# Loading x in pieces of 118 partitions, a scratch array with four rows side by side, and routing lists that stand earlier in the order

## The chip, the cores and the metric

The kernel runs on one core of one Trainium2 chip. The metric is the device time of one execution in microseconds (us). Five engines work side by side, each through its own instructions in order: TensorE (PE, with PEld for its weight loads), VectorE (DVE), ScalarE (ACT), GpSimd (POOL) and SyncE (SP). SP and ACT issue plain DMAs, POOL issues the indexed ones (gather and scatter by row number). All of them are carried out by the core's 16 DMA engines.

## The reference

The reference smooths each sequence with a causal filter and then routes every token to one of eight experts.

```python
# x: (8, 3584, 192) f32, 8 heads of 24 channels, 7 taps per head
w = softmax(weight, axis=-1)
attn[b, s] = sum over k of w[head, k] * x[b, s - 6 + k]        # zeros before s = 0

# 28672 tokens of 192, 8 experts with room for 3584 tokens each
logits = attn @ w_gate                                          # 28672 x 8
# greedy: all (token, expert) pairs by falling logit; a pair is taken
# if the token has no expert yet and the expert still has room
out[token] = relu(attn[token] @ w1[e]) @ w2[e]                  # 192 -> 1024 -> 192
```

Everything is float32. The kernel computes the matrix products of the experts in split halves (a high and a low part of each operand), which is why one product shows as several matmuls.

## The kernel before

**Convolution.** The 28672 tokens are handled in 16 half batches of 1792. A half batch lies in SBUF as a tile `X` of 118 partitions x 16 columns x 192: column w holds the 112 tokens of run w on partitions 6 to 117, and on partitions 0 to 5 the six tokens ahead of them (the halo). `load` (L182 to L192) fills it with two DMAs on SP's queue, one for the six halo partitions and one for the other 112. Each run that such a DMA moves is one token row of 768 bytes. `conv` (L194 to L203) makes one matmul `cv<-X,TH` for each of the 8 heads (TH holds the filter as a band matrix), ACT copies each result to the tile `a`, and a DMA on ACT's queue writes `a` to the scratch array `attn` in DRAM, token by token. There are three buffers for `X` and two for `a`: a load waits for the matmuls that used its buffer, and the copies of half batch i wait until the write of half batch i - 2 has landed.

**Logits.** DVE transposes `a` (`transp`), 48 small matmuls `pl` make the logits, ACT copies them (`L`), PE turns them (`pt`) and DVE writes them to `LT`, with a correction `pm` for columns that hold no token. `end` does the turn and the running maximum (`top`). In the loop the transposes of half batch i - 1 and the logits of i - 2 stand between the matmuls of half batch i.

**Routing in the background.** `Route` makes the lists of token numbers by expert. Its steps are generators, run one after the other by `Steps`, which is asked at many places of the loops (`hook`) whether the next step's input should be there. This is judged by `Pace`, a small clock that adds estimated times of the instructions written so far. The first list (`half(0)`: a threshold, then places, slots, a sort with the one-hot tiles `oa`, a gather by matmul and the numbers `ia0`) covers the first 128 of 256 columns, that is the first eight half batches. `tail` and `tail2` then compute the logits of half batches 14 and 15, and `half(1)`, `rest` and `last` make the other lists during the experts' work.

**Experts.** `FFN` works through 56 tiles of 512 tokens. For each, POOL gathers four times 128 rows of `attn` by the list (L1175), PE transposes them (`px`), `l1` makes eight blocks `ph`, and `l2` sums them to `y`, whose rows POOL scatters to the output (L1243). Weights come through four buffers `raw` (`wload`, SP's queue) and are split by `wsplit` into a high part (ACT) and a low part (POOL or DVE). The first tile's gather stands behind the whole convolution and waits for `ia0`.

The order of each engine is the order in which this program writes its instructions; there is no later scheduler.

Of the kernel before, what the change touches and what calls it, by code (L numbers as in the profile page):

```python
# [16 lines left out]
G = 256  # L17
# [95 lines left out]
def build(ctx, tc, nc, x, weight, wg, attn, LT, wk):  # L113
# [48 lines left out]
    pm = wk.tile([128, 16], F32, name="pm")  # L162

    def gate_ops():
        for pb in range(4):
            nc.sync.dma_start(wgr[32 * pb:32 * pb + 32], wg.rearrange("(c f) e -> f c e", f=32))
        P.memset(GF, 0.0)
        for pb in range(4):
            q = slice(32 * pb, 32 * pb + 32)
            P.tensor_copy(GF[q, :, 8 * pb:8 * pb + 8], wgr[q])  # L170

        pi = cst.tile([128, 1], I32, name="pi")
        P.iota(pi, pattern=[[0, 1]], base=0, channel_multiplier=1)
        V.tensor_scalar(pi, pi, 16, None, op0=OP.bitwise_and)
        V.memset(pm, 0.0)
        for b in range(4):
            V.tensor_scalar(pm[:, 4 * b + 3:4 * b + 4], pi, -1.0 / 16, None, op0=OP.mult)
# [16 lines left out]
    def conv(i, mid):  # L194
# [8 lines left out]
        A.dma_start(attn[i * 1792:(i + 1) * 1792].rearrange("(w p) d -> p w d", p=W), a[0:W])  # L203
# [10 lines left out]
    def transp_last(u):  # L214

        i = NHB - 1
        a = wk.tile([128, 16, 64], F32, name="X%d" % u)
        for q in range(2):
            V.transpose(a[:, 8 * q:8 * q + 8], AA[i][:, 8 * q:8 * q + 8, 64 * u:64 * u + 64])
        AT[i] = AT[i] + [a] if u else [a]  # L220

    def logits(i, u):
# [4 lines left out]
        for c in range(4):  # L227
            w = slice(4 * c, 4 * c + 4)
            t = AT[i][u // 2].rearrange("p w (c t) -> p w c t", t=32)[:, w, u % 2] if i == NHB - 1 else AT[i][0][:, w, u]
            PE.matmul(pl[32 * c:32 * c + 32, 0:128], GF[:, u], t, start=(u == 0), stop=(u == 5))  # L230
# [13 lines left out]
    k.toeplitz, k.gate_ops, k.transp_last = toeplitz, gate_ops, transp_last  # L244
# [4 lines left out]
TA = 12  # L249
# [13 lines left out]
class Route:  # L263

# [268 lines left out]
    def tokens(self, nt, idx, e1=8, t1=None):  # L533
# [10 lines left out]
        i = v(wk.tile([128, 128], I32, name="m_j"))  # L544
        off = wk.tile([128, 1], F32, name="off")
# [16 lines left out]
    def lists(self, F, nt, h, base, idx, *part):  # L562
# [6 lines left out]
        yield from self.tokens(nt, idx, *part)  # L569
# [240 lines left out]
class General:  # L810


    def __init__(self, ctx, tc, ltab, attn, w1, w2, out, ident, drm):
# [4 lines left out]
        self.list = drm.tile([NTOK, 1], I32, name="glist")  # L818

    def consts(self):  # L820
# [20 lines left out]
        self.idi = p.tile([128, G], I32, name="g_idi")  # L841
        V.tensor_copy(self.idi, self.id)
# [131 lines left out]
    def lists(self):  # L974
# [25 lines left out]
        i1 = p.tile([128, 1], I32, name="g_i1")  # L1000
        with tc.For_i(0, G, 1) as g:
            V.tensor_copy(s1, si[:, bass.ds(g, 1)])
            V.tensor_copy(i1, self.idi[:, bass.ds(g, 1)])
# [4 lines left out]
    def ffn(self):  # L1008
# [5 lines left out]
        ix = p.tile([128, 1], I32, name="g_ix")  # L1014
# [7 lines left out]
        with tc.For_i(0, NE, 1) as e:  # L1022
# [3 lines left out]
            with tc.For_i(0, CAP // 128, 1) as t:  # L1026
                nc.sync.dma_start(ix, self.list[bass.ds(e * CAP + t * 128, 128)])
                P.indirect_dma_start(out=x, out_offset=None, in_=self.attn,
                                     in_offset=bass.IndirectOffsetOnAxis(ap=ix, axis=0),
# [15 lines left out]
                P.indirect_dma_start(out=self.out, out_offset=bass.IndirectOffsetOnAxis(ap=ix, axis=0),  # L1045
# [8 lines left out]
class FFN:  # L1054
# [235 lines left out]
    def run(self, idx_of, at, eng, free):  # L1290
# [4 lines left out]
        for i in range(n + 1):  # L1295
            at(i)
            if i + 2 < n:
                self.gather(i + 2, idx_of(tiles[i + 2]))
# [18 lines left out]

NL = 3


def moe_kernel(ctx, tc, x, weight, wg, w1, w2, out):
# [6 lines left out]
    with ExitStack() as cw:  # L1328
# [16 lines left out]

        order = [(e, (0,)) for e in range(NE)]
# [10 lines left out]
        def half(h):  # L1357
# [6 lines left out]
            yield from r.lists(r.F, TA, h, 0 if h else None, *((ia,) if h else (ia0, 8, 4)))  # L1364

        def rest():
# [3 lines left out]
            yield from r.lists(r.F, TB, 1, None, ib0, NL, 4)  # L1370

        def last():
            yield from r.lists(r.F, TB, 0, 1, ib)

        def tail():

            for u in range(6):
                k.logits(14, u)
                if u % 2:
                    yield PEA if u == 5 else None  # L1380
            end(14)
            cs.close()
            ff.wpool2(cw, 1)
            ff.hp[1] = pool(cw, "fh1", 1, **late)
            yield

        def tail2():
# [5 lines left out]
            nc.sync.dma_start(r.ltab, LT)  # L1393
            yield
# [4 lines left out]
        cx = [ExitStack() for _ in range(3)]  # L1399
        k = build(cs, tc, nc, x, weight, wg, attn, LT, wk)  # L1400
# [3 lines left out]
        k.ap = pool(ca, "ap", 2, **right)  # L1404
# [13 lines left out]
        def first(e):  # L1418
# [136 lines left out]
```

## Time and profile before

| | us |
|---|---|
| median of three runs (1328.0 to 1332.42) | 1328.93 |
| the profiled execution, its own time | 1324.88 |
| span of that profile | 1323.1 |
| last write of `attn` issued | 170.06 |
| first matmul of the first expert tile (`ph<-xa,w`) | 181.96 |
| PE busy in the span | 1251.3 |

PE is busy for 95% of the span. Two stages differ: up to about 170 us the convolution runs while 23 MB of x are read and 22 MB of scratch are written, and the DMA engines are nearly always busy; from 182 us on, the experts' matmuls fill PE, and DMA is busy for a quarter to a half of the time. In the page's second part a digit is the busy share of a slice in tenths; a DMA share above 1 in a row of a window means that recorded packets overlap. Packets are counted over all 16 DMA engines of the core.

### The profile page before, as it was taken

What the parts mean: (1) busy time and instruction counts of PE and PEld (TensorE: products, weight loads), DVE (VectorE), ACT (ScalarE), POOL (GpSimd) and SP (SyncE); (2) the same over time, 40 slices, a digit from 0 to 9 for tenths busy, and PEclk for the clock granted to TensorE, in tenths of its full rate; (3) what the DMA queues carried; (4) which work ended last, traced back from release to release, by engine and by line L of the source; (5) the groups of instructions that cost most, each with busy time, mean ns of one, the idle gap of its engine ahead of it and who ended that gap; (6) DMA issues with size and microseconds to landing.
All of it is one profiled execution on the core that took longest, in us unless ns stands there. A gap on an engine that the chain in (4) does not pass through costs nothing.

```text
span 1323.1 us, 21760 instructions
## 1 busy us (share of the span) xinstructions
PE 1251.3 (95%) x7879; PEld 1077.4 (81%) x7879; DVE 1005.2 (76%) x2223; ACT 543.2 (41%) x1182; POOL 540.1 (41%) x547
## 2 busy tenths in 40 slices
PE   5888959999799999999999999999999999999997
PEld 2444637887789888888899999999999999999996
DVE  7369648779999988899757777777777777777772
ACT  4434434475444434443333333333333333333332
POOL 3000065586644434435224434444444444444422
PEclk9889989899899999999899999999999999999999
DMA  9999879488753433424222341432323222141100
GB/s 239 285 294 297 231 211 324 154 275 270 241 186 101 143 99 134 145 91 143 76 83 89 130 160 45 149 101 87 104 87 104 93 93 90 48 148 46 41 29 27
DMA packets 114434, 188.29 MB, mean 142 GB/s; under 512 B 12352, under 2 KB 86544, under 8 KB 110096
## 3 DMA queue, kind: packets, MB, share of 16 engines
q1 hardware_dynamic: 63888, 120.75, 28.4%
q0 software_dynamic: 21504, 44.07, 10.9%
q10 hardware_dynamic: 28928, 22.02, 5.2%
q8 instruction: 63, 1.03, 0.3%
q14 instruction: 51, 0.42, 0.1%
HBM read 114.44 MB, written 72.35 MB: 141 GB/s over the span
## 4 chain that ended last, share of the span: by engine, by line
PE 77%; DVE 9%; DMA 8%; issue 2%; POOL 2%; ACT 2%; SPq 1%; POOLq 0%; ACTq 0%; DVEq 0%
PE ph L54 34%; PE y L54 33%; DMA attn<-a 5%; PE cv L54 4%; PE bg L54 3%; DMA raw<-in_moe_w_dram 3%; DVE X L54 2%; DVE hl L54 2%; PE px L54 1%; PE pl L54 1%; DVE TH L54 1%; DVE oa L54 1%; POOL xg L1175 1%; POOL w L1156 1%; DVE r_w L54 0%
## 5 line engine op out<-in xcount | busy, mean ns | idle before, releaser
L54 PE MATMUL y<-w,hh 128*128 128x384 f32 x1792 | 543.6, 359 | 0.0
L54 ACT ACTIVATE hh<-ph 128x512 fp32r<-128x512 f32 x448 | 267.0, 596 | 492.3 <-PE ph L54 491.9
L54 PE MATMUL y<-w,hl 128*128 128x192 f32 x1792 | 451.3, 252 | 0.0
L54 DVE SCALAR_TENSOR_TENSOR hl<-ph,hh 128x512 fp32r<-128x512 f32 x448 | 308.2, 689 | 174.6 <-ACT hh L54 170.9
L54 PE MATMUL ph<-xa,w 128*128 128x512 f32 x1344 | 399.7, 406 | 2.3 <-DVE hl L54 2.3
L54 PEld LDWEIGHTS y<-w,hh 128*128 128x128 f32 x1792 | 339.4, 189 | 25.2 <-issue 7.5
L54 PEld LDWEIGHTS y<-w,hl 128*128 128x128 f32 x1792 | 344.0, 192 | 15.2
L1243 POOL DMA_INDIRECT out_dram<-yo,ib x128 | 128.0, 1000 | 294.2 <-DVE yo L54 279.4
L54 PEld LDWEIGHTS ph<-xa,w 128*128 128x128 f32 x1344 | 221.5, 191 | 22.7 <-DVE hl L54 2.9
L1243 POOL DMA_INDIRECT out_dram<-yo,ia x96 | 106.3, 1108 | 241.0 <-DVE yo L54 210.3
L54 DVE STREAM_TRANSPOSE xs<-xg 32x256 f32<-32x256 f32 (+1 forms) x512 | 188.8, 369 | 8.8
L54 PE MATMUL ph<-xd,w 128*128 128x512 f32 x448 | 179.7, 401 | 0.0
L54 PE MATMUL ph<-xd,dl 128*128 128x512 f32 x448 | 175.8, 392 | 1.2 <-DVE dl L54 1.2
L1175 POOL DMA_INDIRECT xg<-attn,ib x128 | 129.7, 1013 | 40.1 <-issue 39.8
L54 PE MATMUL cv<-X,TH 118*128 118x384 f32 x256 | 103.8, 539 | 31.1 <-ACT a L54 18.4
L1175 POOL DMA_INDIRECT xg<-attn,ia x96 | 106.8, 1112 | 28.9 <-issue 23.2
L54 ACT ACTIVATE yt<-y 128x192 f32<-128x192 f32 x224 | 73.3, 327 | 108.2 <-PE y L54 105.2
L54 DVE TENSOR_TENSOR yo<-y,yt 128x192 f32<-128x192 f32 x224 | 79.7, 356 | 42.1 <-ACT yt L54 39.3
L54 PEld LDWEIGHTS ph<-xd,dl 128*128 128x128 f32 x448 | 85.1, 190 | 21.6 <-DVE dl L54 2.6
L54 PEld LDWEIGHTS cv<-X,TH 118*128 118x128 f32 x256 | 48.0, 206 | 66.0 <-ACT a L54 26.7
L54 PEld LDWEIGHTS ph<-xd,w 128*128 128x128 f32 x448 | 85.2, 190 | 20.1 <-DVE xd L54 0.7
L54 ACT ACTIVATE a<-cv 128x384 f32<-128x384 f32 x128 | 59.2, 491 | 66.2 <-DMA attn<-a 36.8
(230 smaller groups left out, 966.6 us busy)
## 6 DMA issues: line engine op xcount, KB each, us to landing
w<-kw SPq DMA_DIRECT2D x16, 1536.0 KB
w<-kv SPq DMA_DIRECT2D x16, 1536.0 KB
X<-in_x_dram SPq DMA_DIRECT2D x16, 1344.0 KB
attn<-a ACTq DMA_DIRECT2D x16, 1344.0 KB
kw<-w SPq DMA_DIRECT2D x48, 256.0 KB
kv<-w SPq DMA_DIRECT2D x32, 384.0 KB
raw<-in_moe_w_dram SPq DMA_DIRECT2D x32, 192.0 KB
raw<-in_moe_w_dram SPq DMA_DIRECT2D x16, 256.0 KB
```

The source lines that it names most:

```text
L54: return f(*a, **k)
L1156: eng.tensor_tensor(lo, r[0:n], hi[0:n].bitcast(F32), op=OP.subtract)
L1175: self.nc.gpsimd.indirect_dma_start(out=t[:, b], out_offset=None, in_=self.attn[0:rows], in_offset=bass.IndirectOffsetOnAxis(ap=idx[b], ax ...
L1243: st = nc.gpsimd.indirect_dma_start(out=self.out, out_offset=bass.IndirectOffsetOnAxis(ap=idx, axis=0), in_=o, in_offset=None, bounds_chec ...
```

## The change

**Loads of x.** `load` now moves all 118 partitions at once, in four DMAs of four columns each. In an even half batch, whose first column has no halo in DRAM, that column goes by itself over 112 partitions and the next DMA takes three columns. The same rows as before are moved, 768 bytes each.

**Scratch.** The row order of `attn` becomes: half batch, group of four runs, token within a run, run within the group. So the four columns of a group lie side by side and one run of the write is 3072 bytes. A gather needs the scratch row and the scatter the token number, so `tokens` computes both (`ja`, `ia`), and the slow general path keeps pairs. `a` has three buffers.

**Order.** Transposes and logits of half batch i - 1 stand within half batch i. From half batch 13 on they are held back until the first list is done; `hook` tells `Pace` a time (8.6 per half batch, 11.0 at the start). The first two tiles' gathers are issued as soon as `ia0` and `ja0` are there, and the first tile's transposes stand inside half batch 15. The pools for them are opened at the start. `tail` (half batch 14) is gone from the background, since its logits belong to the loop now; half batch 15 keeps a tail. The first tile's buffer is cleared by POOL, not DVE.

**Small moves.** The correction `pm` is added by ACT when it copies the logits (two copies in place of one), and ACT instead of DVE writes `LT`.

SP's order at the start of the program: `wb` are the filter taps, `X` the half batches, `wgr` the gate weights. Before:

```order
L123 DMA wb<-in_weight_dram 128x56
L188 DMA X<-in_x_dram 6x15x192
L192 DMA X<-in_x_dram 112x16x192
L191 DMA X<-in_x_dram 6x16x192
L192 DMA X<-in_x_dram 112x16x192
L166 DMA wgr<-in_moe_w_gate_dram 32x6x8 x4
```

Now:

```order
L124 DMA wb<-in_weight_dram 128x56
L190 DMA X<-in_x_dram 112x192
L193 DMA X<-in_x_dram 118x3x192
L193 DMA X<-in_x_dram 118x4x192 x7
L167 DMA wgr<-in_moe_w_gate_dram 32x6x8 x4
```

Two half batches take nine DMAs in place of four, and eight of the nine have 118 partitions as their outer count.

POOL's order from its last clearing of `X` to the second tile's weights (`w`, `dl` are low parts of split weights, `xg` the gathered tokens). Before:

```order
L187 MEMSET X 6x192 x4
L1078 MEMSET dl 64x1024
L1156 TENSOR_TENSOR w_1629<-raw,w_1629 128x512
L1156 TENSOR_TENSOR dl<-raw,w_1629 64x512
L1175 DMA xg<-attn,ia_105 128x192 x8
L1156 TENSOR_TENSOR w_1629<-raw,w_1629 128x512
L1156 TENSOR_TENSOR dl<-raw,w_1629 64x512
L1078 MEMSET dl 64x1024
```

Now:

```order
L189 MEMSET X 6x192 x4
L1179 MEMSET xg 128x768
L1181 DMA xg<-attn,ja_109 128x192 x4
L1179 MEMSET xg 128x768
L1181 DMA xg<-attn,ja_109 128x192 x4
L1162 TENSOR_TENSOR w_1622<-raw,w_1622 128x512
L1162 TENSOR_TENSOR dl<-raw,w_1622 64x512
L1162 TENSOR_TENSOR w_1622<-raw,w_1622 128x512
L1162 TENSOR_TENSOR dl<-raw,w_1622 64x512
L1084 MEMSET dl 64x1024
```

The eight gathers of the first two tiles moved ahead of all weight work on POOL.

ACT's order over the last two half batches (`asm` belongs to the first list, `w<-raw` are weights of the first expert). Before:

```order
L54 ACTIVATE asm<-bg 128x192
L54 ACTIVATE a<-cv 128x16x24 x2
L54 ACTIVATE w_1629<-raw 128x512
L54 ACTIVATE a<-cv 128x16x24
L54 ACTIVATE L<-pl 128x128
L54 ACTIVATE w_1629<-raw 128x512
L54 ACTIVATE a<-cv 128x16x24 x3
L203 DMA attn<-a 112x16x192
```

Now, from `asm` to the middle of half batch 14:

```order
L55 ACTIVATE asm<-bg 128x192
L55 ACTIVATE a<-cv 128x16x24 x3
L204 DMA attn<-a 112x4x768
L55 ACTIVATE a<-cv 128x16x24
L55 ACTIVATE w_1622<-raw 128x512
L55 ACTIVATE a<-cv 128x16x24 x2
L55 ACTIVATE w_1622<-raw 128x512
L55 ACTIVATE a<-cv 128x16x24 x2
L55 ACTIVATE L<-pl 128x4x16
L55 ACTIVATE L<-pl,pm 128x4x16
L55 ACTIVATE w_1622<-raw 128x512
```

The last matmul of the first list moved from half batch 15 to half batch 13, and the copies of half batch 14 now stand behind weights that come through `raw`.

The core of the diff:

```diff
@@ load
+        x_ = lambda w, n, p: bass.AP(tensor=x.tensor, offset=o + (w * W + p - 6) * D, ap=[[D, 118 - p], [W * D, n], [1, D]])
+
+        parts = [(4 * c, 4) for c in range(4)]
         if hf == 0:
             P.memset(t[0:6, 0], 0.0)
-            nc.sync.dma_start(t[0:6, 1:16], bass.AP(tensor=x.tensor, offset=o + (W - 6) * D,
-                                                    ap=[[D, 6], [W * D, 15], [1, D]]))
-        else:
-            nc.sync.dma_start(t[0:6], bass.AP(tensor=x.tensor, offset=o - 6 * D, ap=[[D, 6], [W * D, 16], [1, D]]))
-        nc.sync.dma_start(t[6:118], bass.AP(tensor=x.tensor, offset=o, ap=[[D, W], [W * D, 16], [1, D]]))
+            nc.sync.dma_start(t[6:118, 0:1], x_(0, 1, 6))
+            parts[0] = (1, 3)
+        for w, n in parts:
+            nc.sync.dma_start(t[:, w:w + n], x_(w, n, 0))
@@ conv
-        A.dma_start(attn[i * 1792:(i + 1) * 1792].rearrange("(w p) d -> p w d", p=W), a[0:W])
+        A.dma_start(attn[i * 1792:(i + 1) * 1792].rearrange("(g p b) d -> p g (b d)", g=4, b=4),
+                    a[0:W].rearrange("p (g b) d -> p g (b d)", b=4))
@@ logits, logits_t
-            A.activation(L, pl[:, 0:128], AF.Copy)
+            l, m = (t.rearrange("p (w t) -> p w t", t=32) for t in (L, pl[:, 0:128]))
+            A.activation(l[:, :, 0:16], m[:, :, 0:16], AF.Copy)
+            A.activation(l[:, :, 16:32], m[:, :, 16:32], AF.Identity, bias=pm)
...
-        V.tensor_tensor(o, v, pm.rearrange("p (b q) -> p b q", q=4)[:, None].to_broadcast([128, 8, 4, 4]), op=OP.add)
+        A.activation(o, v, AF.Copy)
@@ tokens
+        V.scalar_tensor_tensor(y, i, -127.0 / 4, x, op0=OP.mult, op1=OP.add)
...
+        V.scalar_tensor_tensor(y, gi, 28.0, y, op0=OP.mult, op1=OP.add)
...
+        V.scalar_tensor_tensor(y, i, 4.0, y, op0=OP.mult, op1=OP.add)
+        V.tensor_scalar(row, y, 4.0, None, op0=OP.mult)
@@ moe_kernel
+PERIOD, START = 8.6, 11.0
+LAG = 13
...
-        bg = Steps(nc, r, (half(0), tail(), tail2(), half(1), rest(), last()))
-        bg.keep = 5
+        bg = Steps(nc, r, (half(0), tail(), half(1), rest(), last()))
+        bg.keep = 4
...
-        k.ap = pool(ca, "ap", 2, **right)
+        k.ap = pool(ca, "ap", 3, **right)
...
+        def steps(i):
+
+            def gate(u):
+                if u == 3:
+                    return end(i)
+                for f in range(2 * u, 2 * u + 2):
+                    k.logits(i, f)
+
+            return [partial(k.transp, i, u) for u in range(4)] + [partial(gate, u) for u in range(4)]
+
+        def hook(at):
+            nc.pe = max(nc.pe, PERIOD * at / 8 + START)
             bg.hook(1.5)
-            if len(bg.gens) == 5:
-                gather()
+            if not got and len(bg.gens) == 4:
+                first()
+                got.append(at)
+            elif got and at >= got[0] + 10 and at % 8 in (2, 5) and todo:
+                for _ in range(2):
+                    todo.pop(0)()
...
             def mid(h):
-                if i and h < 4:
-                    k.transp(i - 1, h)
-                if 2 <= i and h in (2, 5):
-                    for u in range(3):
-                        k.logits(i - 2, h // 4 * 3 + u)
-                if i == 15 and h in (4, 5):
+
+                if i and h == 0:
+                    left.extend(steps(i - 1))
+                for _ in range(2 if got else 1):
+                    if left and (i < LAG or got):
+                        left.pop(0)()
+                    if not left or left[0].func != k.transp:
+                        break
+                if i >= 14 and h % 2:
                     ff.wsplit(-1, P)
...
```

More of the change, by code (lines that the diff above doesn't have):

```diff
@@ L568, in lists @@
         yield from self.gather(nt, base is None)
-        yield from self.tokens(nt, idx, *part)
+        yield from self.tokens(nt, idx, row, *part)
     def counts(self, n0):
@@ L1369, in rest @@
             yield from r.final(NL)
-            yield from r.lists(r.F, TB, 1, None, ib0, NL, 4)
+            yield from r.lists(r.F, TB, 1, None, ib0, jb0, NL, 4)
         def last():
-            yield from r.lists(r.F, TB, 0, 1, ib)
+            yield from r.lists(r.F, TB, 0, 1, ib, jb)
         def tail():
[L1377 to L1387, printed above, removed]
             for u in range(6):
@@ L1490, in moe_kernel, with idx_of @@
         ff.op = pool(cw, "fo", 3, **late)
+        ff.xp = pool(cw, "fp", 1, **late)
         ff.hp = [pool(cw, "fh0", 1, **late), None]
         ff.wpool(cw, 1)
-        def idx_of(tile_):
+        def idx_of(tile_, rows=False):
             e, t = tile_[1]
             if t == 0:
-                return [ia0[:, e, b:b + 1] for b in range(4)]
+                return [(ja0 if rows else ia0)[:, e, b:b + 1] for b in range(4)]
             if t < 3:
@@ L1500, in idx_of @@
                     bg.drain(2)
-                return [ia[:, e, 4 * t + b:4 * t + b + 1] for b in range(4)]
+                return [(ja if rows else ia)[:, e, 4 * t + b:4 * t + b + 1] for b in range(4)]
             if t == 3 and e < NL:
```

118 lines of the change are left out of this document (55 added, 63 removed).

## The prediction

> **What bounds the kernel now.** I read the span in windows first, by stage (columns: engine busy times with their counts, granted TensorE clock, DMA share, GB/s).
>
> ```profile
> 10.00:30.00 20.00, 17.19 (x64) 8.93 (x64) 16.75 (x51) 9.30 (x21) 6.36 (x28) 1.00 1.07 250
> ...
> 110.00:130.00 20.00, 16.61 (x151) 9.00 (x149) 18.45 (x35) 7.69 (x19) 1.20 (x2) 0.98 1.09 308
> ...
> 150.00:170.00 20.00, 18.72 (x223) 12.64 (x221) 16.28 (x39) 11.79 (x25) 2.33 (x2) 1.00 0.64 195
> 170.00:182.00 12.00, 2.49 (x10) 1.61 (x10) 0.96 (x3) 0.63 (x2) 8.45 (x9) 0.64 0.84 247
> ```
>
> ```profile
> 300.00:600.00 300.00, 289.02 (x1677) 257.37 (x1676) 275.62 (x650) 136.99 (x337) 144.37 (x133) 0.98 0.47 158
> ```
>
> Up to 130 us the DMA share stands at about 1: the convolution is bound by its transfers. From 300 us on PE is busy for 289 of 300 us and DMA for half. So the program is a DMA stage, a gap, and a PE stage that nothing shortens; the time moves with the moment at which the PE stage starts. The timeline around the gap, ACT's last write of the scratch, the first gather on POOL, the first transposes on PE and the first expert matmul:
>
> ```profile
> 170.06 0.31 ACTq L203 DMA_DIRECT2D attn<-a  x1
> ...
> 170.39 1.25 POOL L1175 DMA_INDIRECT xg<-attn,ia  x1 [0.17 <-issue]
> ...
> 179.50 1.75 PE L54 MATMUL px<-ident,xg 128*128 128x128 f32 x4 [9.99 <-DMA xg<-attn,ia]
> ...
> 181.96 1.63 PE L54 MATMUL ph<-xa,w 128*128 128x512 f32 x3
> ```
>
> The experts start at 181.96, and 1323.1 - 181.96 = 1141 us follow. What ended the waits in the DMA stage, in the view of waits for 20 to 170 us:
>
> ```profile
> ACT a L54 <- DMA attn<-a: 36.8, 8, 9.3
> ```
>
> ACT stood 36.8 us for a free buffer `a`, that is for writes.
>
> **How many DMA engines a load uses.** This decides the case. The two rows are the packets of the first 4.3 us, and of ACT's queue (which carries only the 16 scratch writes) over the whole span.
>
> ```profile
> DMA packets 507, 0.30 MB, mean 70 GB/s; under 512 B 150, under 2 KB 507, under 8 KB 507
> ```
>
> ```profile
> q10 hardware_dynamic: 28928, 22.02, 5.2%
> ```
>
> 28928 is 28672 rows and 256 more: 16 for each of the 16 writes, so I read them as one short closing packet per engine used, and a DMA over 112 partitions uses 16. In the first 4.3 us the short packets are 150: 128 runs of the filter taps, and 22 closings, which are 16 for the taps (128 partitions) and 6 for the first halo load (6 partitions). So the outer count is cut over the engines, and whole partitions stay on one: 90 runs of 768 bytes went over six engines, not sixteen. Every count that this program cuts (6, 32, 64, 112, 128) can be cut into equal shares on 6 or 16 engines. The new count cannot: 118 is 2 x 59. If shares must be equal, it goes to two engines. If shares may differ, it goes to fifteen or sixteen. No row of before holds an uneven cut, so the trace leaves both open; since all that it shows is equal, I give equal shares eight in ten.
>
> The Trainium skill speaks against this change: "DMA: Bandwidth & Descriptors", section "Why a DMA increments its semaphore by 16 and not by 1", says that the sync and scalar queues use the largest number of engines, up to 16, that divides the outermost counts of both sides; it names 100 partitions, which give 10, and 127, which give 1. By that rule 118 gives 2, the same sum as below; the trace agrees with it for 6 and 112, and no run here shows an uneven count.
>
> **The change, part by part.** *Loads.* In an even half batch 15 columns of 118 rows go to the two engines (885 packets each) and one column of 112 rows to all (7 each): 892. In an odd one 16 columns: 944. Over 8 of each, 8 x (892 + 944) = 14688 packets of 768 bytes on each of the two. The price of one, from rows where reading and writing fill the engines, and where reading fills them alone:
>
> ```profile
> 30.00:32.00 2.00, 0.00 (x0) 1.00 1.10 373
> ```
>
> ```profile
> DMA packets 6122, 3.97 MB, mean 198 GB/s; under 512 B 1026, under 2 KB 6122, under 8 KB 6122
> ...
> q1 hardware_dynamic: 6122, 3.97, 94.2%
> ```
>
> At 373 GB/s an engine moves 23.3 GB/s, a row in 33 ns. Over ACT's queue the mean is 0.052 x 16 x 1323.1 us / 28928 = 38 ns. In the first 20 us, where sixteen engines read at once, it is 0.942 x 16 x 20 us / 6122 = 49 ns. Two engines read far less at once than sixteen, so the first is nearest: 14688 x 33 ns = 484 us. Ends: 33 ns, and 38 ns (559 us); 49 ns belongs to a load on the memory that two engines cannot make.
>
> *Scratch writes.* Their 112 partitions still give 16 engines, so the two busy ones carry a sixteenth: 22.02 MB / 16 = 1.38 MB, at 23.3 GB/s 59 us. Longer runs may make it less, the 38 ns price per 768 bytes makes it 69 us; nothing at all would need the write to ride in gaps of an engine that has none, which I keep as the low end. Sum: the loads begin at 2 us, so the last half batch is in SBUF at 2 + 484 + 59 = 545 us (486 to 630).
>
> *The end of the convolution.* SP issues the first expert's `raw` loads behind the last load of x, so on the two busy engines they land behind it, and ACT's copies of half batch 14 stand behind `w<-raw`. After 545 us ACT has 15 copies of `cv`, four of `w` and some logits left, at the pace and prices of these rows:
>
> ```profile
> 22.82 0.49 ACT L54 ACTIVATE a<-cv 128x384 f32<-128x384 f32 x1 [0.15 <-PE cv L54]
> 23.46 0.49 ACT L54 ACTIVATE a<-cv 128x384 f32<-128x384 f32 x1 [0.15 <-PE cv L54]
> ...
> 168.08 0.28 ACT L54 ACTIVATE L<-pl 128x128 f32<-128x128 f32 x1 [0.72 <-PE pl L54]
> 168.25 0.62 ACT L54 ACTIVATE w<-raw 128x512 fp32r<-128x512 f32 x1
> ```
>
> ```profile
> 148.44 2.10 PE L54 MATMUL cv<-X,TH 118*128 118x384 f32 x6
> ...
> 160.51 0.31 PE L54 MATMUL pt<-ident,L 128*128 128x128 f32 x1
> ...
> 167.15 0.86 PE L54 MATMUL pl<-aT,c_mu 128*32 128x128 f32 x24
> ...
> 167.94 1.56 PE L54 MATMUL cv<-X,TH 118*128 118x384 f32 x4
> ```
>
> 15 x 0.64 + 4 x 0.62 = 12 us, with three half batches' `L` and `LT` (about 0.3 each) and the first tile's two copies 15 us. The low end is 10, the copies alone; the high end 21 is what half batches 14 and 15 took before (148.44 to 169.5 on PE, with a list between). Then 24 logit matmuls (0.86) and a turn (0.31), 1.2 us. The experts start at 561 us in place of 182: 379 us later (315 to 470).
>
> *Everything else is covered by this wait.* The rows for it, from the timeline:
>
> ```profile
> 160.85 0.29 DVE L54 TENSOR_TENSOR LT<-pt,pm 128x128 f32<-128x128 f32 x1 [1.92 <-PE pt L54]
> ...
> 167.02 0.19 DVE L54 SCALAR_TENSOR_TENSOR ia<-m_j,m_x 128x32 int32<-128x32 int32 x1
> 167.11 1.29 POOL L1156 TENSOR_TENSOR w<-raw,w 128x512 fp32r<-128x512 f32 x1 [42.39 <-ACT w L54]
> ...
> 168.22 1.50 DVE L54 MEMSET xg<- 128x768 f32 x2
> ...
> 179.76 1.00 POOL L1175 DMA_INDIRECT xg<-attn,ia  x1 [0.30 <-issue]
> ```
>
> Third buffer: a half batch now takes 543 / 16 = 34 us, so no copy waits for a write, and the 36.8 us are gone without showing. Lists: they end with half batch 13; the eight gathers (170.39 to 180.76, 10.4 us) pass on POOL while two half batches of x, 68 us, are outstanding. The held logits of 12 and 13, ACT's second `L`, its writing of `LT` (0.29 us each on DVE before), POOL's clearing (1.5 us on DVE before) and four DVE operations of some 0.2 us more per list: all inside the same wait, or beside PE in the second stage. Without that cover they are worth what the first rival says. *The PE stage* stays 1141 us, give or take 5: its order is the same but for half batch 14's 24 matmuls.
>
> Against the profiled execution: 1324.88 + 379 = 1704 us. The median of the runs shown lies 4.05 us higher, so 1708.
>
> **Rivals.** *Uneven shares.* If fourteen engines take 8 partitions each and one 6, the busiest carries 128 rows per half batch. The old loads put just that on six engines (7 rows of the 112 and one halo partition, 16 columns), so loading costs what it did: 2048 x 33 to 49 ns = 67 to 100 us, writes 59, in all 128 to 161 with the start. Then the rest of the change counts. The third buffer takes away a good half of 36.8 us, so the convolution ends near 150, not 169.5. The list, whose numbers were there at 167.2, 2 us ahead of the end, is ready two half batches sooner, about 19 us ahead; its gathers (10.4), two clearings (1.5) and POOL's two low parts (1.29 each) take 15. So the experts start at about 151: 31 us earlier, 1298. For it: nothing forbids uneven shares in a row. Against it: no row shows one.
>
> *Pairs that change.* If each of the four pieces takes another pair, eight engines read: 14688 x 2 / 8 = 3672 packets x 33 ns = 121 us, with 59 us of writes 180. The experts start near 198: +16, 1345. The halo loads tell nothing on which engines they took.
>
> *Earlier lists that are not earlier*, with uneven shares. DVE was busy for 18.45 of 20 us from 110 to 130; if it cannot take the list's one-hots sooner, the gathers still end the gap, and the start is at 179: 1326, no change.
>
> **Numbers.** Equal shares on two engines 0.80, uneven shares 0.14, changing pairs 0.04, late lists 0.02. The forecast is the first, 1708 us. Its own range is 1324.9 + 315 and + 470, with 4 added: 1644 to 1799, rounded to 1640 and 1800; this leaves out the other cases, two in ten. A change of 0.3% (4 us) is about what a measurement tells: faster 0.14, same 0.02, slower 0.04 + 0.80 = 0.84.
>
> **What would show it.** Right: in the first 30 us of the new profile DMA moves about 47 GB/s at a share near one eighth; `PE cv` waits for the load of X some 30 us per half batch; the first `ph` stands near 560; from there 1141 us follow; the gathers land long ahead. Two-engine shares but another price would move the start alone: each 1 ns per packet is 15 us. Wrong: a DMA share near 1 in the first 20 us means that 118 partitions spread, and the first rival's chain holds; about half of that means changing pairs.

## The result

| | before | the change |
|---|---|---|
| median of six runs each | 1330.74 us (1328.0 to 1332.42) | 1720.91 us (1718.05 to 1725.14) |
| span of the profiled execution | 1323.1 us | 1723.3 us |
| first expert matmul `ph` | 181.96 us | 578.51 us |
| from there to the end of the span | 1141.1 us | 1144.8 us |

The ratio is 1.294, with a 95% interval of 1.291 to 1.297: 29% slower. The forecast was 1708 us, 13 us below the measured time, and the range 1640 to 1800 us holds it. Of the 400 us by which the span grew, 397 lie ahead of the first expert matmul.

The windows of the changed kernel (columns as in the prediction: engine busy times with their counts, granted TensorE clock, DMA share, GB/s):

```profile
10.00:30.00 20.00, 0.00 (x0) 0.00 (x0) 8.42 (x31) 1.31 (x4) 2.15 (x6) 1.00 0.14 45
...
100.00:200.00 100.00, 31.40 (x195) 15.62 (x195) 14.59 (x24) 13.22 (x33) 1.23 (x2) 0.62 0.25 83
...
300.00:400.00 100.00, 32.04 (x238) 17.23 (x238) 24.42 (x42) 13.29 (x34) 0.25 (x1) 0.65 0.25 83
...
600.00:900.00 300.00, 284.63 (x1728) 252.54 (x1729) 263.40 (x578) 149.62 (x362) 163.96 (x147) 0.97 0.60 197
```

Between 10 and 30 us, where before the DMA share was 1.07, it is now 0.14, which is 2.2 engines of 16, at 45 GB/s instead of 250. Through most of the convolution PE is busy for about a third of the time. After 600 us the picture is that of the kernel before.

What ended the waits in the first 600 us (engine, what it wanted, who ended it: us in total, times, longest):

```profile
ACT a L55 <- PE cv L55: 363.7, 79, 26.4
PE cv L55 <- DMA X<-in_x_dram: 347.9, 14, 35.6
```

PE waits for a load of x 14 times, 25 us on average and up to 35.6; ACT waits for PE. The wait of ACT for its writes, 36.8 us before, is not in the list. The packets at a moment when nothing but x is moved (530 to 540 us), and the queues of the whole execution (packets, MB, share of 16 engines):

```profile
DMA packets 588, 0.45 MB, mean 45 GB/s; under 512 B 2, under 2 KB 588, under 8 KB 588
```

```profile
q1 hardware_dynamic: 63792, 120.75, 20.7%
...
q10 hardware_dynamic: 7424, 22.02, 3.7%
```

588 packets in 10 us on two engines are 294 each: **34.0 ns a packet**. The scratch writes shrank from 28928 packets to 7168 runs of 3072 bytes and the same 256 closings.

The end of the convolution on PE, and on ACT (columns: start, duration, instruction, count, idle time before it and what ended it):

```profile
519.25 5.46 PE L55 MATMUL cv<-X,TH 118*128 118x384 f32 x8 [24.49 <-DMA X<-in_x_dram]
...
544.21 1.65 PE L55 MATMUL cv<-X,TH 118*128 118x384 f32 x2 [18.53 <-ACT a L55]
...
557.29 1.65 PE L55 MATMUL cv<-X,TH 118*128 118x384 f32 x2 [10.41 <-ACT a L55]
...
578.51 1.63 PE L55 MATMUL ph<-xa,w 128*128 128x512 f32 x3
```

```profile
494.80 0.49 ACT L55 ACTIVATE a<-cv 128x384 f32<-128x384 f32 x1 [0.15 <-PE cv L55]
543.24 0.31 ACTq L204 DMA_DIRECT2D attn<-a  x1
543.67 0.49 ACT L55 ACTIVATE a<-cv 128x384 f32<-128x384 f32 x1 [48.38 <-DMA X<-in_x_dram]
556.23 0.63 ACT L55 ACTIVATE w<-raw 128x512 fp32r<-128x512 f32 x1 [12.07 <-DMA raw<-in_moe_w_dram]
...
573.72 0.31 ACTq L204 DMA_DIRECT2D attn<-a  x1
```

PE starts half batch 14 at 519, but then stands behind ACT, which has two waits of its own. Its copies of half batch 13 end at 495.3; then it stands 48.4 us in front of the write of half batch 13, until a load of x has landed. Later it stands 12 us for the first expert's weights. The first wait comes from the program. The semaphores (counters by which a DMA reports that it has landed) of these plain DMAs are eight, shared in turn by the loads on SP and the writes on ACT (numbers 100 to 107 in the trace, DMAHW0 to DMAHW7 in the program), and a DMA waits until the one before it with the same semaphore has landed. The write of half batch 13 has number 100, and so has the load of x that landed at 543.2 us, just before the write was issued. The order of instructions shows the rule: the ninth to eleventh DMA on SP's queue, and one of ACT's writes, with the semaphores for which they wait:

```
L193 DMA X<-in_x_dram 118x4x192 [waits DMAHW0_49]
L193 DMA X<-in_x_dram 118x4x192 [waits DMAHW1_49]
L167 DMA wgr<-in_moe_w_gate_dram 32x6x8 [waits DMAHW2_49]
...
L204 DMA attn<-a 112x4x768 [waits DMAHW0_49,Activation_49]
```

The semaphores also tell when a load lands. Those of the last load of x get their counts from its two engines at 552.7 and 555.6 us. So the last x is in SBUF at 555.6 us, and the experts start 22.9 us behind it.

### The profile page after: what moved, and what is told of

The parts are those of the page before. It is cut to its first block, busy times and chain, and to the rows that moved or that the text cites. A ratio compares the mean times of both kernels' runs of the same rounds, so it can differ in the third digit from the quotient of the medians.

```text
span 1723.3 us, 21868 instructions
## 1 busy us (share of the span) xinstructions
PE 1288.1 (75%) x7879; PEld 1092.0 (63%) x7879; DVE 1001.1 (58%) x2215; ACT 545.8 (32%) x1214; POOL 538.7 (31%) x549
## 3 DMA queue, kind: packets, MB, share of 16 engines
q1 hardware_dynamic: 63792, 120.75, 20.7%
q10 hardware_dynamic: 7424, 22.02, 3.7%
## 4 chain that ended last, share of the span: by engine, by line
PE 55%; DVE 6%; issue 2%; ACT 1%; POOL 1%; DMA 1%; another core or an unknown queue 0%; SPq 0%; POOLq 0%; DVEq 0%; ACTq 0%
PE ph L55 26%; PE y L55 26%; PE bg L55 2%; DVE X L55 2%; DVE hl L55 1%; PE px L55 1%; DMA raw<-in_moe_w_dram 1%; POOL w L1162 0%; DVE yo L55 0%; ACT a_d L55 0%; DVE r_w L55 0%; DVE oa L55 0%; ACT hh L55 0%; DVE r_no L55 0%
## 5 line engine op out<-in xcount | busy, mean ns | idle before, releaser
L55 PE MATMUL cv<-X,TH 118*128 118x384 f32 x256 | 136.7, 674 | 397.7 <-DMA X<-in_x_dram 347.9
L55 PEld LDWEIGHTS cv<-X,TH 118*128 118x128 f32 x256 | 61.2, 263 | 443.2 <-issue 407.8
L1181 POOL DMA_INDIRECT xg<-attn,jb x128 | 129.7, 1013 | 40.1 <-issue 39.8
L1181 POOL DMA_INDIRECT xg<-attn,ja x96 | 105.5, 1099 | 98.3 <-issue 93.4
L55 DVE TENSOR_REDUCE M<-LT 128x16 f32<-128x128 f32 x16 | 5.9, 369 | 196.8 <-ACT LT L55 196.8
L55 DVE TENSOR_TENSOR yo<-y,yt 128x192 f32<-128x192 f32 x224 | 79.5, 355 | 40.1 <-ACT yt L55 36.8
```

The lines of the kernel that those rows point to most:

```text
L55: return f(*a, **k)
L1181: self.nc.gpsimd.indirect_dma_start(out=t[:, b], out_offset=None, in_=self.attn[0:rows], in_offset=bass.IndirectOffsetOnAxis(ap=idx[b], ax ...
```

## Experiments on the main cause

In the results below, "times before" is the ratio to the kernel before as it was measured beside that run; its median in the three groups of runs was 1323.36, 1328.47 and 1327.0 us. In the cuts of code, `...` stands for what is left out.

**The old load in the change.** Only `load` goes back to before:

```diff
-        for w, n in parts:
-            nc.sync.dma_start(t[:, w:w + n], x_(w, n, 0))
+        nc.sync.dma_start(t[0:6], ...)        # 6 partitions x 16 columns
+        nc.sync.dma_start(t[6:118], ...)      # 112 partitions x 16 columns
```

> The change with the loads of before put back: one load of 6 partitions and one of 112 per half batch; all the rest of the change stays. Theory A (the whole slowdown is that a load of 118 partitions is cut over two DMA engines): the first 30 us move some 200 to 250 GB/s again, and the time is that of the first rival of the prediction, 1298 us (1290 to 1310), some 31 us faster than before. Rival B (the slowdown comes from another part: the write with longer runs, the third buffer, the eight-fold order of DMAs): well over 1400 us. Rival C (the earlier lists give nothing): 1326 us, within 0.3% of before.

1327.26 us, 1.0024 times before (interval 1.0005 to 1.0042). The slowdown is the load's. But the 31 us of the first rival did not come either: the number is that of rival C, and the section on the rest of the change asks why.

**The 118-partition load in the kernel before**, in one piece:

```diff
-        nc.sync.dma_start(t[0:6], ...)
-        nc.sync.dma_start(t[6:118], ...)
+        nc.sync.dma_start(t[:, 0:16], x_(0, 16, 0))   # 118 partitions; even half batches: 112 for column 0, 118 for 15
```

> The kernel before, with one thing changed: a half batch is loaded by one transfer over 118 partitions (even half batches: 112 partitions for the first column, 118 for the other fifteen) in place of 6 and 112. Not cut into four. Theory A: two engines, 42 to 47 GB/s in the first 30 us; 14688 packets per engine at 34 ns are 501 us, writes some 40 to 59 more, so the experts start near 560 to 590 and the time is 1700 to 1735 us. Rival B (cutting the load into four transfers is what costs): 1320 to 1340 us, as before.

One run, 1726.9 us, beside 1323.36 for the kernel before. Its window, and the queue of the loads:

```profile
10.00:30.00 20.00, 0.00 (x0) 0.00 (x0) 8.40 (x31) 1.28 (x4) 2.12 (x6) 1.00 0.14 45
```

```profile
q1 hardware_dynamic: 63696, 120.75, 20.8%
```

The same 0.14 and 45 GB/s. The count alone is enough; the cutting into four, the longer writes and the order are not needed for it.

**Four pieces, but 6 and 112 partitions:**

```diff
-            nc.sync.dma_start(t[:, w:w + n], x_(w, n, 0))
+            nc.sync.dma_start(t[0:6, w:w + n], ...)
+            nc.sync.dma_start(t[6:118, w:w + n], ...)
```

> The change with its four pieces of columns kept, but each piece loaded by two transfers, one of 6 and one of 112 partitions. Theory A (only the partition count matters): the first 30 us at 200 GB/s or more, and about the time of the change with the old load, 1298 us (1290 to 1315). Theory A with a price for the number of transfers (the trace of the change shows ACT and SP standing until a transfer issued eight earlier has landed; here there are nine per half batch, so less than one half batch can be under way): the convolution loses 2 to 4 us per half batch, 1330 to 1360 us. Rival B (the four pieces are the cause): well over 1400 us.

1332.75 us, 1.008 (1.0053 to 1.0107): no slowdown of that size, and 5.5 us above the old load with two transfers. The price of many transfers, if that is it, is at the low end of what was expected.

**X made 120 partitions high:**

```diff
-        t = X[i] = k.xp[i % 3].tile([118, 16, D], F32, name="X")
+        t = X[i] = k.xp[i % 3].tile([120, 16, D], F32, name="X")
-        V.tensor_scalar(MK[:, j], D0[:, 0:W], float(j), None, op0=OP.is_equal)
+        V.tensor_scalar(MK[:, j], D0[:, 0:W], float(j + 2), None, op0=OP.is_equal)
...
+        nc.sync.dma_start(t[:, 0:16], x_(0, 16, 0))   # 120 partitions; even half batches: 112 for column 0, 120 for 15
...
+            PE.matmul(ps[:, 0:384], TH[0:120, h], t[:, :, h * 24:(h + 1) * 24], start=True, stop=True)
```

> The change with X made 120 partitions high (two more rows of halo, the band matrix shifted by two), so that a half batch is one transfer over 120 partitions (even ones: 112 for the first column and 120 for the other fifteen). Equal shares: 15 engines of 8 partitions, 128 packets each per half batch, as many as the six busiest engines carry before; 200 GB/s or more in the first 30 us, DMA share near 0.94 where transfers bind; 1298 us (1285 to 1310), the same within 5 us as with the old load. If a count over 112 is what sends a transfer to two engines, whatever it divides by: 1700 us or more.

1333.21 us, 1.0089 (1.0059 to 1.012): a count above 112 is no harm in itself. It came out some 6 us above the old load, where I had expected the same within 5. It reads 496 rows more, and between 10 and 30 us it moved 211 GB/s where the old load moved 266. It has the fewest transfers and the experiment before it the most, and both are slower than the old load by about the same; so the number of transfers is not shown to be what costs this.

**114 and 4 partitions:**

```diff
-            nc.sync.dma_start(t[:, w:w + n], x_(w, n, 0))
+            nc.sync.dma_start(t[0:114, w:w + n], ...)
+            nc.sync.dma_start(t[114:118, w:w + n], ...)
```

> The change with each half batch loaded by two transfers, one over 114 partitions and one over 4 (even half batches: the first column apart, as in the change). 114 is 6 x 19. Theory A (the number of engines is the largest count up to 16 that divides the partitions): six engines carry 19 partitions each and four of them one more, 320 packets per half batch, 5120 in all; at 34 ns 174 us, at 38 ns 195 us, with 40 to 59 us of writes the last x lands at 216 to 256 us and the experts start some 31 us later, 1395 to 1430 us. If any count that 16 does not divide goes to two engines: 1700 us or more. If any even count over 112 spreads: 1320 to 1335 us.

One run, 1393.5 us. Its packets from 10 to 20 us, where only x is moved:

```profile
DMA packets 1741, 1.34 MB, mean 134 GB/s; under 512 B 10, under 2 KB 1740, under 8 KB 1740
```

134 GB/s is three times the 45 of the two engines, so six work, at the same 22 GB/s each; the last x lands at 227.6 us and the experts start at 251.3, both where theory A had them; the time is 1.5 us below its range. With 118, 120 and 114 partitions going to two, fifteen and six engines (counted below), the number of engines follows the divisors of the count, not its size, and the sum over packets per engine carries over.

**Counting closings.** The packets of SP's queue give the sum of the engines used. Whole executions of before, of four pieces of 6 and 112, of 120 and of 114 and 4:

```profile
q1 hardware_dynamic: 63888, 120.75, 28.4%
```

```profile
q1 hardware_dynamic: 65072, 120.75, 28.0%
```

```profile
q1 hardware_dynamic: 64400, 121.13, 29.6%
```

```profile
q1 hardware_dynamic: 63824, 120.75, 25.8%
```

Before, the 32 loads close with 16 x (16 + 6) = 352 packets. If 118 closes with 2, the change has 8 x (16 + 4 x 2) + 8 x 4 x 2 = 256, which is 96 fewer: 63792, as measured. One piece of 118: 160, so 63696, as measured. Eight transfers of 6 and 112: 1536, so 65072. 114 with 6 and 4 with 4: 288, so 63824. 120 with 15: 368, and 496 more rows of x: 64400. All five agree to the packet. The semaphores say it load by load: a load of 118, 114, 120, 112, 6 and 4 partitions gets 2, 6, 15, 16, 6 and 4 counts as it lands, and one more when it is issued if fewer than sixteen engines work. The Trainium skill's rule ("DMA: Bandwidth & Descriptors", section "Why a DMA increments its semaphore by 16 and not by 1": the largest number up to 16 that divides the outermost counts of both sides) gives 2, 6, 4, 15, 16 and 6 for 118, 114, 4, 120, 112 and 6; every one of them is in these counts.

**The writes' price.** The change with each scratch write issued twice, the second time into rows that nobody reads:

```diff
+    K.twin = drm.tile([NTOK, D], F32, name="twin")
...
+        A.dma_start(K.twin[i * 1792:(i + 1) * 1792].rearrange("(g p b) d -> p g (b d)", g=4, b=4),
+                    a[0:W].rearrange("p (g b) d -> p g (b d)", b=4))
```

> The change (four pieces over 118 partitions) with every scratch write issued twice, the second into rows that nobody reads. It tells what the writes cost on the two engines that carry the loads. Theory A1 (they take those engines' time): another 22.02 MB, a sixteenth per engine, costs as much as the first did, 40 to 59 us, so about 1760 to 1780 us. Theory A2 (writes ride in gaps between the reads, and a read costs 37 ns): 1720 to 1730 us.

One run, 1768.21 us. Its span and the write queue:

```profile
span 1766.4 us, 21890 instructions
...
q10 hardware_dynamic: 14848, 44.04, 7.3%
```

The span is 1766.4 - 1723.3 = 43 us longer for 22.02 MB more. So writes take the busy engines' time (A1): 448 runs of 3072 bytes per engine in 43 us, 96 ns each. The trace of the change itself gives much the same: from 80 to 100 us, without a write, 1174 rows of x pass, and from 100 to 120 us, with one whole write, 987. At 34.0 ns on two engines the 187 rows are 3.2 us for one write.

**Weights early.** The change with the first four weight loads issued at half batch 8:

```diff
             if i == 13:
                 cx[1].close()
+            if i == 8:
                 for _ in range(4):
                     ff.wload()
```

> The change with one thing moved: the first four weight loads (raw) are issued with half batch 8 instead of 13, so they land long before the convolution ends. In the change the experts start 31 us after the last x, not 16; ACT stands 12.07 us there for raw. Theory: that wait was on the path; without it the experts start near 566 us in place of 578, 1707 to 1714 us. Rival (the copies, logits and transposes of half batches 14 and 15 set the end, not raw): 1718 to 1724 us.

One run, 1719.36 us: the time of the rival. The wait for weights is gone, and ACT has made all copies of half batch 14 and its four of `w` by 537 us. But half batch 15 starts late instead:

```profile
561.43 2.90 PE L55 MATMUL cv<-X,TH 118*128 118x384 f32 x4 [25.63 <-DMA kd<-dl]
...
577.70 0.94 PE L55 MATMUL ph<-xa,w 128*128 128x512 f32 x3
```

(The profile names the transfer that landed last; what this matmul reads is X.) The last x lands at 561.3 us here, 5.7 us later than in the change: the write of half batch 14 and further weights now pass the two busy engines ahead of it. From there to the experts it is 16.4 us in place of 22.9; the 31 us of the expectation counted from too early a landing. The two differences cancel, and the start is 577.7 against 578.5. That the two engines must carry the same either way, and that this is why the start stays, is a reading that no run tests by itself.

## Experiments on the rest of the change

With the loads put right the rest should have gained 31 us; it lost 3 to 4. Up to its first expert matmul (190.47 us, before 181.96), the kernel with the old load spends on PE, and before that the kernel before (columns: busy us, mean ns | idle time just ahead, and what ended it):

```profile
L54 PE MATMUL cv<-X,TH 118*128 118x384 f32 x256 | 103.8, 539 | 31.1 <-ACT a L54 18.4 <-DVE TH L54 12.0 <-POOL X L187 0.4
L54 PE MATMUL pl<-aT,c_mu 128*32 128x128 f32 x672 | 26.7, 297 | 0.0
```

```profile
L55 PE MATMUL cv<-X,TH 118*128 118x384 f32 x256 | 106.0, 543 | 11.6 <-DMA X<-in_x_dram 11.3 <-DVE TH L55 0.3
L55 PE MATMUL pl<-aT,c_mu 128*32 128x128 f32 x720 | 47.3, 304 | 18.3 <-DVE aT L55 18.1
```

The first block is before, the second the change with the old load. The wait for `a` (18.4 us) has gone, as it should. In its place the logit matmuls `pl` wait 18.1 us for DVE's transposes `aT` and are busy for 47.3 us instead of 26.7, in small groups with gaps. The change moved each half batch's logits one half batch ahead, right behind its own transposes.

**Logits one half batch later again** (old load kept):

```diff
-                    k.logits(i, f)
+                    k.logits(i - 1, f)
...
-            return [partial(k.transp, i, u) for u in range(4)] + [partial(gate, u) for u in range(4)]
+            t = [partial(k.transp, i, u) for u in range(4)] if i < NHB - 1 else []
+            g = [partial(gate, u) for u in range(4)] if i else []
+            return t[0:2] + g[0:1] + t[2:3] + g[1:2] + t[3:4] + g[2:4]
-        for f in left + todo:
+        for f in left + todo + steps(NHB - 1):
```

> The change with the old load, and the logits of a half batch moved one half batch behind its transposes again (in convolution i: transposes of i-1, logits of i-2), as in the kernel before. With the old load alone the convolution was not faster than before: up to the first expert matmul PE spent 47.3 us on the logit matmuls (pl) and waited 18.3 us for their transposes (aT), where before it spent 26.7 and waited 0. Theory P (that wait is what took the gain of the third buffer): pl falls back to 27 to 32 us with almost no wait, the convolution and so the experts start 15 to 35 us earlier, 1295 to 1315 us. Rival L (the list sets the start, whatever PE waits for): the gathers stay near 165 us and the time at 1320 to 1330 us.

1315.34 us, **0.989 times before (0.984 to 0.995)**. The same rows, and the experts' first matmul (first and last start):

```profile
L55 PE MATMUL cv<-X,TH 118*128 118x384 f32 x256 | 104.5, 535 | 23.9 <-DVE TH L55 12.6 <-DMA X<-in_x_dram 8.8 <-ACT a L55 2.5
L55 PE MATMUL pl<-aT,c_mu 128*32 128x128 f32 x720 | 29.4, 286 | 0.0
```

```profile
L55 PE MATMUL ph<-xa,w x1344: 388/397/794, 174.2 to 1291.3; 128*128 128x512 f32 x192
```

`pl` is back at 29.4 us without a wait, and the experts start 16 us earlier than with the old load alone. Theory P holds, at the low end of its 15 to 35 us and 0.3 us above its range of times. Of the idle time left ahead of `cv`, 12.6 us are the building of the filter at the start.

Against the kernel before, though, the convolution has not become shorter. ACT issues its last write at 170.47 us, where before it was 170.06 (with the old load alone 186.43):

```profile
149.33 0.18 DVE L55 TENSOR_SCALAR ja<-m_y 128x32 int32<-128x32 f32 x1
155.09 1.25 POOL L1179 DMA_INDIRECT xg<-attn,ja  x1 [0.30 <-POOL xg L1177]
170.47 0.36 ACTq L202 DMA_DIRECT2D attn<-a  x1
```

What is gained is the gap behind it: the first list's numbers come at 149.3 us instead of 167.0, the gathers pass within the convolution, and the experts start 3.7 us after the last write instead of 11.9.

Three parts of the change were then taken out one at a time. The base of two of them lets nothing be held back:

```diff
-LAG = 13
+LAG = 16
```

> The change with the old load and the later logits (the faster version of this study), and without its holding back of transposes and logits from half batch 13 on (LAG 16 in place of 13). It is the base of the next two. What is held are a few logits of half batches that pass beside the gathers; 1310 to 1320 us, within 0.4% of the version with the hold. If the hold was what lets the list through in time: 1320 to 1330 us.

1320.22 us, 0.994 (0.9914 to 0.9967): at the upper end of what was expected, and not clearly apart from the version with the hold, since the two intervals overlap. Two buffers `a`:

```diff
-        k.ap = pool(ca, "ap", 3, **right)
+        k.ap = pool(ca, "ap", 2, **right)
```

> The same without the hold, and with two buffers a in place of three. Theory (the third buffer is a part of the gain, since ACT stood 36.8 us for writes before): ACT waits for attn<-a again, 15 to 35 us in all, and the time is 8 to 20 us above the version without the hold, 1322 to 1335 us. Rival (with longer runs the writes are quick enough, or PE is the bound by now): within 5 us of it.

1317.62 us, 0.9923 (0.9896 to 0.995): the rival. Its waits from 20 to 175 us:

```profile
ACT a L55 <- DMA attn<-a: 22.5, 8, 6.0
PE cv L55 <- ACT a L55: 6.7, 5, 3.3
```

ACT does wait for its writes again, but only 6.7 us of that reach PE. Gathers behind the convolution:

```diff
-            if not got and len(bg.gens) == 4:
+            if False:                              # first() then runs behind the loop
```

> The same without the hold, three buffers, and with the eight gathers and the first tile's transposes behind the convolution instead of within it, as before. Theory (the gap of 10 us before the experts was the gathers' time): PE stands some 8 to 10 us for xg again, 1322 to 1332 us. Rival (the gathers would have to wait for the list or the writes of half batch 7 anyway, or the held PE work fills the gap): within 4 us.

1318.61 us, 0.9928 (0.9902 to 0.9954): the rival again. PE waits for the gathered rows, but little (waits from 20 to 175 us):

```profile
PE bg L55 <- DMA xg<-attn,ja: 3.5, 3, 2.4
```

The edit moves the gathers less than its words say. They stand behind the loop in the program, but the list is done at 152.7 us and POOL starts them at 162.2, which is 7 us later than in the base and still 5 us ahead of the last write of `attn`. So a start as late as before (170.4 us) was not tried here.

The scratch rows of before, in the version with later logits:

```diff
-        A.dma_start(attn[...].rearrange("(g p b) d -> p g (b d)", g=4, b=4), a[0:W].rearrange("p (g b) d -> p g (b d)", b=4))
+        A.dma_start(attn[...].rearrange("(w p) d -> p w d", p=W), a[0:W])
...
-            ff.gather(e, [ja0[:, e, b:b + 1] for b in range(4)], NTOK // 2, P)
+            ff.gather(e, [ia0[:, e, b:b + 1] for b in range(4)], NTOK // 2, P)
```

> The faster version (old load, later logits, with the hold) with the scratch rows of before: a write is 16 runs of 768 bytes per partition instead of 4 runs of 3072, and the gathers use the token numbers as rows. On the two engines of the change a 3072-byte run cost about 96 ns more engine time (43 us for 448 of them); four of 768 at 36 ns are 144 ns, so the 16 writes take some 21 us more of each engine. If transfers still bind the convolution: 10 to 20 us slower than the faster version, 1325 to 1335 us. If PE binds it: within 4 us of it, 1312 to 1319 us.

1312.3 us, 0.989 (0.9854 to 0.9926): no difference from the longer runs. Here the experts start at 166.8 us, 7 us earlier than with the longer runs, yet the stage behind them takes 1144 us instead of 1137, and the time is the same. What gives the earlier start back in the experts' stage was not found. Over the versions with the old load that stage lasts 1136 to 1146 us, and it tends to be longer where the experts start earlier; so a few us of an earlier start need not show in the time.

So two versions beat the kernel before by 1.1%. Taken out alone, neither the third buffer nor the longer runs change the time there by more than the runs scatter, and nor do the gathers when they start 7 us later. What remains in common between the faster versions and against the kernel before (the list one to two half batches earlier, the logits of half batch 14 out of the experts' way, ACT's share of the small work) was not taken apart further.

## Why the prediction was right, step by step

- **How many DMA engines a load uses.** Equal shares on two engines, given 0.80: shown, by the counts of closings, by the 0.14 share, and by 114 and 120. The pairs do not change either: two or three of the pieces are under way at a time (one is issued every 8 us and lands some 20 us later), and still only two engines' worth is busy.
- **14688 packets at 33 ns, 484 us.** Right in count; the price was 34.0 ns, so 500 us. The choice of row was right (the busiest moment of all engines, not the read-only start at 49 ns), 3% low. The packet records themselves last longer than that, since they overlap; the rate is what counts.
- **Scratch writes, 59 us.** Mis-sized. They take 43 us by the doubled writes, because a run of 3072 bytes costs 96 ns, not four times 33. The prediction had said "Longer runs may make it less" and not priced it. The low end of 0, writes riding in gaps, is excluded by the doubled writes.
- **The last x at 545 us.** It landed at 555.6. With the measured prices, 2 + 500 + 43 is again 545 us; that the two errors cancel is luck, and 10.6 us are missing from the sum. Some 5 of them go, for the most part, to the first weights. The prediction let them land behind the last x, and so gave them no time; in the trace they pass between its last rows. Packets from 540 to 542 us, and from 550 to 552 us:

```profile
DMA packets 118, 0.09 MB, mean 45 GB/s; under 512 B 1, under 2 KB 118, under 8 KB 118
```

```profile
DMA packets 353, 0.58 MB, mean 291 GB/s; under 512 B 45, under 2 KB 98, under 8 KB 353
```

  Rows of x are those under 2 KB without those under 512 B: 117 in the first 2 us, 53 in the second. From 548 us on the last 137 rows take 7.6 us in place of 2.3. The rest was not taken apart by a run; the eight gathers, which the sum leaves out too, and the 3.2 us that a write takes in the change's own trace may be most of it.
- **The end of the convolution, 15 + 1.2 us.** Also mis-sized: 22.9 us. When the last x landed, ACT had just the 15 copies of `cv` and the four of `w` ahead of it that the prediction counted. It had stood 48.4 us in front of a write, where the prediction had not looked at the semaphores for which DMAs wait, and then 12.07 us for weights, which came at 556.2 us, 0.6 us after the last x. The last copy ended at 573.7 us, so they took 18.1 us, not 15. Then 4.8 us passed, not 1.2: the 1.2 priced 24 logit matmuls and a turn, and gave no time to DVE's transposes, for which PE waits, nor to the 24 further matmuls `pl`. That the version with early weights shows 16.4 us, nearly the 16.2 of the sum, bears nothing out: only eight copies were left there.
- **The PE stage, 1141 us give or take 5.** 1144.8.
- **Everything else is covered by this wait.** In the change, yes. The first and the last of the eight gathers:

```profile
496.94 1.25 POOL L1181 DMA_INDIRECT xg<-attn,ja  x1 [69.63 <-issue]
...
507.03 1.00 POOL L1181 DMA_INDIRECT xg<-attn,ja  x1 [0.30 <-issue]
```

  They pass 70 us ahead of the experts.
- **"Without that cover they are worth what the first rival says."** Wrong. The rival had the experts at 151 us and 1298 us in all. With loads that spread they start at 190 and the time is 1327. The step that failed is "The third buffer takes away a good half of 36.8 us, so the convolution ends near 150": with the old load the last write is issued at 186.4 us, and the list's numbers come 2.3 us sooner than before, not two half batches. The wait did go, but the logits' move ahead, which I had not costed, put a wait for `aT` in its place; with the logits later again the experts start 16 us earlier. Nor was the wait worth so much: with two buffers, 6.7 us of it reach PE.

The total was 13 us low: 10.6 us from the landing of the last x, 6.7 from the end of the convolution and 4 from the PE stage, less 8, because the median lies 4 us below the profiled execution's own time (1725.14 us), where I had put it 4 above.

## What to carry to other kernels

Look at the outer count of every plain DMA that moves much: a count like 118 leaves fourteen of sixteen engines idle. Joining two transfers of 6 and 112 partitions into one cost about 30% here, while cutting them into eight cost less than 1%. Count the short closing packets of a queue, or take GB/s in a window with one kind of transfer and divide by that of one engine, to see how many engines work. When a wait is taken away by a buffer, look in the new order for an instruction that now stands right behind its producer, since that wait can take its place.

## What the runs showed of the hardware that was not expected

Two DMA engines by themselves read rows of 768 bytes at 34.0 ns each (45 GB/s, 22.5 GB/s an engine), and six at the same rate (134 GB/s). In the first 20 us of the kernel before, where sixteen read at once, it was 198 GB/s, which is 12.4 GB/s an engine. (The 49 ns of the prediction for these 20 us counts 1026 short packets in; over the other 5096 packets the same busy time is 59 ns each.) With writes beside the reads, sixteen engines reached 373 GB/s at 30 to 32 us. So reads by few engines seem to be held by the engines, and reads by all sixteen by something that they share; no run tests what that is.

The granted TensorE clock was 0.62 to 0.65 in the windows above in which PE was busy for 31 to 32 us of 100, and 0.97 where it was busy for 285 of 300. (Before PE's first matmul, from 10 to 30 us, the row says 1.00.) A convolution matmul took 674 ns on average against 539 before (first 600 us of the change):

```profile
L55 PE MATMUL cv<-X,TH 118*128 118x384 f32 x256 | 136.7, 674 | 397.7 <-DMA X<-in_x_dram 347.9 <-ACT a L55 28.9 <-issue 20.8
```

For most of the convolution this cost nothing, because PE was waiting for x anyway. Whether it cost something behind the last x, where from 540 to 560 us the granted clock was 0.50, no run shows.
